# Turning every second pass of a GLU round and keeping its last weights in SBUF, in a kernel that runs attention and GLU side by side

## The chip, the cores and the metric

One core of a Trainium2 chip runs the kernel. The metric is the device time of one execution in microseconds (us), the median of several runs. The core has five engines with queues of their own: TensorE (PE) for matmuls, VectorE (DVE), ScalarE (ACT), GpSimd (POOL), and SyncE (SP), which here issues nearly all DMA transfers. Each engine works its queue in the order in which the kernel wrote the instructions.

## What is computed

The input x has 2048 tokens of 576 values. It is normalised (layer norm without weights), and goes through two branches that meet at the end:

```python
xn = _layernorm(x)
q, k, v = heads(xn @ wqkv)                      # 32 heads of 18
s = softmax(q @ k.T * 18 ** -0.5) @ v           # per head
s = join(s) @ wo
h = (xn @ w_gate) * (xn @ w_up)                 # 4608 wide
g = silu(h @ w_down)
return x + s * g
```

All of it is float32. The kernel splits each factor of a product into a part that the fast float32 form of the matmul holds and a rest, and adds three products (high by high, rest by high, high by rest).

## The kernel before

**Stages.** A first stage of some 300 us makes xn, q, k and v and puts them into DRAM scratch. A last one of some 75 us multiplies by wo and joins the branches. Between them, for some 2400 us, the scores of 32 heads and the whole GLU run interleaved on TensorE. The change touches this stage alone.

**The GLU.** It goes in four passes (`NCH`), one for each 512 tokens. A pass takes the 4608 hidden columns in 18 units (`NF2`) of 256; `units` lists the 72 pairs of pass and unit. A unit has two gate/up tiles n = 2u and 2u + 1 of 128 columns (`gw`, 1152 KB each with gate, up, and their rests, two buffers) and one down tile (`dw`, 1152 KB, one buffer). In the first pass the raw weights are loaded, split by ACT and POOL and stored to scratch (`swg`, `swd`), in later ones the split tiles are loaded from there. `g_get(n + 2)` is called where tile n's gate product ends, `d_get(u + 1)` where unit u's down sums end, and both issue their load on SP at once.

x of a pass lies in SBUF as 18 blocks (`xg`, 4.7 MB in all). In the last gate/up tile of a pass each block is overwritten with the next pass's as soon as it was used for the last time, first in one half of the partitions, then in the other (`x_block`).

**Two streams.** TensorE's rows are used in two halves. Stream 0 works in rows 0 to 63: the up products, half of the down columns, and the score tiles that find the row maxima (`a_item`: 512 keys, then a maximum on DVE). Stream 1 works in rows 64 to 127: the gate products, the other down columns, and the transposed scores (`b_item`: then an Exp on ACT). `visit` puts the products of probabilities and v between them. `stream(r)` yields the matmuls of one stream in their fixed order: two gate/up tiles of 27 matmuls (`TERMS`), then the down sums of the unit before, 4 x 12 matmuls (`DTERMS`).

**The planner.** `order()` decides, while the program is written, in which order all this stands on TensorE's queue. It holds a clock for each stream (`clk`), the times at which DVE and ACT come free (`free`), at which PSUM banks come free (`banks`), and one model of the DMA queue (`queue`): `moved(start, size)` says when `size` MB will have landed, at 0.26 MB per us and 2 us more. `can_go` lets a matmul be written only where the plan has its data there: `loaded` (gate/up tiles), `downed` (down tiles), `there` (x blocks and the products h). What a stream may not do is filled with scores; the scores have due times by the plan's clock (`a_goal`, `b_goal`, `PACE`). Stores, loads of heads and other small transfers are in the model in part only. The plan's times are not in the program: TensorE simply waits where data is late.

**Silu.** Two sets of sums (`acc`) serve four passes. When the four 128-token tiles of a pass are summed up, each one's silu is queued in `later` as seven pieces: an Exp on ACT (`first`), an add on DVE (`second`), four reciprocals of 144 columns on DVE (`inverse`), and a product on POOL with a store to scratch (`last`). They share one buffer, so a tile's Exp needs the store before it. `small(now)` is asked at every step of the planner. It writes the next piece if 6 us of plan time have passed since the last one (`quiet`) and if the piece's engine is free within 0.1 us. Two passes later the sums are overwritten; there `down_end` calls `ready(sdone, ...)`, which writes all pieces that are still missing, one after the other, without asking.

Of the kernel before, what the change touches and what calls it, by code (L numbers as in the profile page):

```python
# [20 lines left out]
FT = mybir.dt.float32  # L21
# [19 lines left out]
def kernel(  # L41
# [10 lines left out]
    nc = tc.nc  # L52
# [6 lines left out]
    NCH = S // 512  # L59
    NF2 = F // 256  # L60
# [14 lines left out]
    swd = dram.tile([NF2, 128, 2, 2, 2, HALF], FT, name="swd")  # L75
# [74 lines left out]
    chores, later = [], []  # L150
# [15 lines left out]

    units = [(c, p) for c in range(NCH) for p in range(NF2)]
    graw, gw, draw, dw = {}, {}, {}, {}  # L170
    gdone, ddone = set(), set()

# [4 lines left out]
    def g_get(n):  # L177

        if n == 2 * len(units):
            u = n // 2 - 1  # L180
            dw[u] = wpool.tile([128, 2, 2, 2, HALF], FR, name="wdl", tag="wgu", bufs=2)
            nc.sync.dma_start(dw[u].bitcast(FT), swd[u % NF2])
            ddone.add(u)
        if n >= 2 * len(units):
            return
        f = n % (2 * NF2)
        w = gw[n] = g_tile()
        if n >= 2 * NF2:
            nc.sync.dma_start(w.bitcast(FT), swg[f])
            gdone.add(n)  # L190
            return
        if n not in graw:
            ready(gdone, n - 2)
        raw = graw.pop(n)

        def piece(b):
            nc.scalar.activation(w[:, b:b + 3, :], raw[:, b:b + 3, :], AF.Copy)  # L197
            nc.gpsimd.tensor_tensor(w[:, 9 + b:12 + b, :], raw[:, b:b + 3, :], w[:, b:b + 3, :].bitcast(FT),  # L198
                                    op=OP.subtract)

        def end():
            gdone.add(n)
            nc.sync.dma_start(swg[f], w.bitcast(FT))
            g_load(n + 2)

        chores.extend([(piece, (b,)) for b in (0, 3, 6)] + [(end, ())])
# [5 lines left out]
    def d_get(n):  # L212
        if n >= len(units) - 1:
            return
        p = n % NF2
        w = dw[n] = d_tile()
        if n >= NF2:
            nc.sync.dma_start(w.bitcast(FT), swd[p])
            ddone.add(n)
            return  # L220
        raw = draw.pop(n)

        def piece(k):
            nc.scalar.activation(w[:, k, :, 0, :], raw[:, k], AF.Copy)  # L224
            nc.gpsimd.tensor_tensor(w[:, k, :, 1, :], raw[:, k], w[:, k, :, 0, :].bitcast(FT), op=OP.subtract)  # L225

        def end():
            ddone.add(n)
            nc.sync.dma_start(swd[p], w.bitcast(FT))
            d_load(n + 1)  # L230

        chores.extend([(piece, (k,)) for k in range(2)] + [(end, ())])
# [236 lines left out]
    with ExitStack() as mid:  # L469
# [148 lines left out]
            return acc[k][t % 4]  # L618

        def down_end(r, u, s, ps):  # L620
            c, p = units[u]
            cs = slice(r * HALF, (r + 1) * HALF)
            if p == 0 and c >= 2:
                ready(sdone, 4 * c - 8 + s)
            a = sums(4 * c + s)[:, cs]
            if p == 0:
                nc.vector.tensor_copy(a, ps[:, 0:HALF])  # L627
            else:
                nc.vector.tensor_tensor(a, a, ps[:, 0:HALF], op=OP.add)  # L629
            if p == NF2 - 1 and c < NCH - 1:  # L630
                seen[c, s] = seen.get((c, s), 0) + 1
                if seen[c, s] == 2:
                    silu_store(4 * c + s)
            if s == 3:
                seen[u] = seen.get(u, 0) + 1
                if seen[u] == 2:
                    d_get(u + 1)
# [46 lines left out]
        def stream(r):  # L684

            for u in range(len(units) + 1):
                for n in (2 * u, 2 * u + 1):
                    if u == len(units):
                        break
                    c, p = units[u]  # L690
                    box = []
                    for k in range(len(TERMS)):
                        def work(n=n, k=k, box=box, c=c, p=p):
                            if k == 0:
                                box.append(gu_start(r, n))
                            gu_op(r, n, box[0], k)
                            if p == NF2 - 1 and n % 2 and k % 3 == 2 and c < NCH - 1:
                                x_block(c + 1, k // 3, (64 * r,))
                                there["x", c + 1, k // 3, r] = moved(clk[r] + 0.5, 0.262)
                            if k == len(TERMS) - 1:  # L700
                                (gate_end if r else up_end)(n, box[0])
                                if r and n == 2 * len(units) - 1:
                                    wo_prepare()
                        end = (("DVE", 0.70) if r else ("ACT", 0.60)) if k == len(TERMS) - 1 else None
                        yield 0.229, k == 0, work, end, ("g", n, k)
                for s in range(4):
                    if not u:
                        break
                    box = []
                    for k in range(len(DTERMS)):  # L710
                        def work(s=s, k=k, box=box, u=u - 1):
                            if k == 0:
                                box.append(down_start(r, u))
                            down_op(r, u, s, box[0], k)
                            if k == len(DTERMS) - 1:
                                down_end(r, u, s, box[0])
                        end = ("DVE", 0.46) if k == len(DTERMS) - 1 else None
                        yield 0.131, k == 0, work, end, ("d", u - 1, 12 * s + k)
# [9 lines left out]
        clk, free = [0.0, 0.0], {"DVE": 0.0, "ACT": 0.0}  # L728
# [11 lines left out]

        def moved(start, size):

            queue[0] = max(queue[0], start) + size / 0.26
            return queue[0] + 2.0

        due, jobs, rows_done = [], [], {}
        there, queue = {}, [0.0]
# [54 lines left out]
        quiet = [0.0]  # L802

        def small(now):

            q = chores or later
            if q is later and now < quiet[0]:
                return
            if q:
                eng, length = KINDS.get(q[0][0].__name__, ("POOL", 0.0))  # L810
                if eng == "POOL" or free[eng] <= now + 0.1:
                    if eng != "POOL":
                        engine(eng, now, length)
                    if not chores:
                        quiet[0] = now + 6.0
                    chore()
# [39 lines left out]
        def can_go(r, first, ev):  # L856

            kind, n, k = ev
            now = clk[r]
            if kind == "d":  # L860
                return k or (there.get(("h", n), 1e9) <= now and (n < 1 or downed.get(n - 1, 1e9) <= now))
            u = n // 2
            c, p = units[u]
            if k == 0 and n > 1 and loaded.get(n - 2, 1e9) > now:
                return False
            if k == 0 and r and gone[0] - gone[1] < FIRST and heads[0] is not None:
                return False
            if k == len(TERMS) - 1:
                if r and upped.get(n, 1e9) > now + 0.3:
                    return False  # L870
                if not r and n > 1 and gated.get(n - 2, 1e9) > now + 0.3:
                    return False
            if c and p == 0 and n % 2 == 0:
                return there.get(("x", c, k // 3, r), 1e9) <= now
            return True

# [16 lines left out]
        def order():  # L893
# [5 lines left out]
            while any(heads) or na < TOTAL or nb < TOTAL or due or jobs:  # L899
                now = max(clk)  # L900
# [26 lines left out]
                elif op is not None:  # L927
# [8 lines left out]
                    if end:  # L936
                        done = engine(end[0], clk[r] + 0.22, end[1])
                        banks["g"][slots[r]] = done + 0.06
                        if kind == "d":
                            if k == 47:  # L940
                                parts.setdefault(n, []).append(clk[r])
                                if len(parts[n]) == 2:
                                    downed[n] = moved(max(parts[n]) + 0.3, 1.18)
                        elif r == 0:
                            upped[n] = done
                        else:
                            gated[n] = done
                            fin = engine("ACT", done + 0.1, 0.63)
                            loaded[n] = moved(done - 0.4, 1.18)
                            lands = moved(fin + 1.3, 0.524)  # L950
                            if n % 2:
                                there["h", n // 2] = lands
# [116 lines left out]
```

## Time and profile before

| | us |
|---|---|
| median of 3 runs (2808.34 to 2814.45) | 2813.01 |
| the profiled execution | 2809.35 |
| its span, first to last instruction | 2807.6 |
| PE busy | 2699.6 |
| DVE busy | 1966.2 |
| ACT busy | 1497.9 |
| POOL busy | 438.2 |

The profile is that of one execution. Busy is the time in which an engine had at least one instruction at work; matmuls of the two streams overlap, so TensorE can be busy with one stream as with both. A number behind an x is a count of instructions. PEclk is TensorE's granted clock as a share of 2.4 GHz, DMA the mean busy share of the 16 DMA engines. The DMA engines moved 522.87 MB, 186 GB/s over the span.

### The profile page before, as it was taken

To read this page: it belongs to the slowest core of one execution; us is meant where nothing else is said; L and a number is where in the kernel's file an instruction comes from. 1 tells how busy PE (TensorE), PEld (TensorE's weight loads), DVE (VectorE), ACT (ScalarE), POOL (GpSimd) and SP (SyncE) were. 2 spreads that over 40 slices of the span, in tenths; PEclk is the share of its full clock that TensorE was granted. 3 is DMA by queue.
4 is the path that set the end of the run, shared out by engine and by line. 5 is a ranking of instruction groups with operands and counts; after the bars stand their busy time and mean duration, and the time that the engine had idled before them with its cause. 6 is when DMAs were issued, how large, how long until landed. Compare 5 with 4: busy or idle time off the path is not lost.

```text
span 2807.6 us, 59270 instructions
## 1 busy us (share of the span) xinstructions
PE 2699.6 (96%) x24600; PEld 2165.5 (77%) x24600; DVE 1966.2 (70%) x3362; ACT 1497.9 (53%) x2765; POOL 438.2 (16%) x405
## 2 busy tenths in 40 slices
PE   7988999999999999999988999999988999999999
PEld 6876877777867877778766777777866777777769
DVE  6214777777767777777766777777767777777436
ACT  3221366666655555556554555555544555555642
POOL 2101433333320001001001000010001000100105
PEclk9998999999999999999998999999998999999989
DMA  7768978789786656565684555565685555654446
GB/s 233 262 198 247 249 213 220 209 217 244 212 225 176 174 157 181 155 182 165 164 212 132 172 162 169 158 174 161 185 203 154 157 166 162 189 157 147 156 144 207
DMA packets 210990, 522.87 MB, mean 186 GB/s; under 512 B 67200, under 2 KB 128672, under 8 KB 176160
## 3 DMA queue, kind: packets, MB, share of 16 engines
q1 hardware_dynamic: 208480, 510.82, 64.3%
q0 software_dynamic: 2240, 8.26, 0.8%
q8 instruction: 193, 3.16, 0.5%
q14 instruction: 77, 0.63, 0.1%
HBM read 330.17 MB, written 112.79 MB: 158 GB/s over the span
## 4 chain that ended last, share of the span: by engine, by line
PE 88%; DMA 7%; DVE 2%; SPq 1%; issue 1%; ACT 0%; POOL 0%; POOLq 0%; ACTq 0%; DVEq 0%
PE pg L573 32%; PE pg L532 16%; PE pg L601 14%; PE pa L487 12%; PE pb L521 7%; PE pg L1026 2%; DMA xc<-sx 2%; DMA wgu<-swg 2%; PE pa L318 1%; PE pg L373 1%; PE pb L318 1%; PE pb L547 1%; DMA qs<-sqk 1%; DVE xn L280 1%; DMA sqk<-hl 0%
## 5 line engine op out<-in xcount | busy, mean ns | idle before, releaser
L573 PE MATMUL pg<-xc,wgu 64*128 64x512 f32 x7776 | 1636.8, 395 | 41.6 <-DMA wgu<-swg 17.8
L523 ACT ACTIVATE pt<-pb 128x512 f32<-128x512 f32 x2048 | 1177.6, 596 | 740.2 <-PE pb L521 571.7
L489 DVE TENSOR_REDUCE mx<-pa 128x1 f32<-128x512 f32 x2048 | 1364.7, 686 | 206.3 <-PE pa L487 123.0
L573 PEld LDWEIGHTS pg<-xc,wgu 64*128 64x128 f32 x7776 | 1172.4, 188 | 99.7 <-DMA wgu<-swg 18.3
L601 PE MATMUL pg<-wd,hs 64*128 64x288 f32 x6816 | 1012.4, 295 | 14.0 <-DVE acc L627 14.0
L601 PEld LDWEIGHTS pg<-wd,hs 64*128 64x128 f32 x6816 | 946.7, 187 | 41.7 <-issue 16.2
L521 PE MATMUL pb<-qs,ks 56*128 56x512 f32 x2048 | 804.3, 409 | 7.1 <-DMA qs<-ml 5.5
L487 PE MATMUL pa<-ks,qs 54*128 54x512 f32 x2048 | 806.3, 405 | 0.8 <-DVE mx L489 0.6
L532 PE MATMUL pg<-pt,vt 128*32 128x512 f32 x4096 | 486.2, 602 | 6.4 <-ACT pt L523 6.3
L487 PEld LDWEIGHTS pa<-ks,qs 54*128 54x128 f32 x2048 | 371.8, 186 | 148.5 <-issue 111.1
L589 POOL TENSOR_TENSOR hs<-us,hs 128x512 fp32r<-128x512 f32 x144 | 185.7, 1290 | 1848.2 <-ACT hs L588 1767.4
L521 PEld LDWEIGHTS pb<-qs,ks 56*128 56x128 f32 x2048 | 365.5, 185 | 23.5 <-issue 5.6
L538 DVE TENSOR_TENSOR oc<-oc,pg 128x512 f32<-128x512 f32 x161 | 110.7, 687 | 335.9 <-PE pg L532 335.8
L532 PEld LDWEIGHTS pg<-pt,vt 128*32 128x32 f32 x4096 | 114.2, 110 | 245.9 <-issue 230.1
L629 DVE TENSOR_TENSOR acc<-acc,pg 128x288 f32<-128x288 f32 x544 | 240.4, 450 | 88.4 <-PE pg L601 74.8
L588 ACT ACTIVATE hs<-us 128x512 fp32r<-128x512 f32 x144 | 91.0, 632 | 154.6 <-DVE us L585 154.6
L198 POOL TENSOR_TENSOR wgu<-wraw,wgu 128x384 fp32r<-128x384 f32 x108 | 108.2, 1013 | 206.0 <-ACT wgu L197 183.6
L585 DVE TENSOR_TENSOR us<-pg,us 128x512 f32<-128x512 f32 x144 | 98.6, 685 | 20.6 <-PE pg L573 9.0
L578 ACT ACTIVATE us<-pg 128x512 f32<-128x512 f32 x144 | 85.9, 597 | 36.3 <-PE pg L573 31.6
L225 POOL TENSOR_TENSOR wd<-draw,wd 128x576 fp32r<-128x576 f32 x36 | 51.3, 1429 | 101.5 <-ACT wd L224 88.5
L1026 PE MATMUL pg<-wos,oT 128*128 128x288 f32 x448 | 63.1, 297 | 0.0
L1026 PEld LDWEIGHTS pg<-wos,oT 128*128 128x128 f32 x448 | 59.9, 188 | 0.3 <-ACT oT L1007 0.3
(99 smaller groups left out, 999.5 us busy)
## 6 DMA issues: line engine op xcount, KB each, us to landing
wgu<-swg SPq DMA_DIRECT2D x108, 1152.0 KB
hs<-hs SPq DMA_DIRECT2D x288, 256.0 KB
wd<-swd SPq DMA_DIRECT2D x53, 1152.0 KB
swg<-wgu SPq DMA_DIRECT2D x36, 1152.0 KB
qs<-sqk SPq DMA_DIRECT2D x192, 144.0 KB
ks<-sqk SPq DMA_DIRECT2D x192, 144.0 KB
swd<-wd SPq DMA_DIRECT2D x18, 1152.0 KB
sqk<-hl SPq DMA_DIRECT2D x32, 512.0 KB
```

Source lines behind the costliest of these rows:

```text
L198: nc.gpsimd.tensor_tensor(w[:, 9 + b:12 + b, :], raw[:, b:b + 3, :], w[:, b:b + 3, :].bitcast(FT), op=OP.subtract)
L487: nc.tensor.matmul(p, q[rows, t * 128:(t + 1) * 128], k[rows, c * 512:(c + 1) * 512], start=True, stop=True)
L489: nc.vector.tensor_reduce(mx[h][:, t, c:c + 1], p, axis=AX.X, op=OP.max)
L521: nc.tensor.matmul(p, k[rows, t * 128:(t + 1) * 128], q[rows, c * 512:(c + 1) * 512], start=True, stop=True)
L523: nc.scalar.activation(pt[t, c // 2][:, c % 2, :], p, AF.Exp, scale=scale)
L532: nc.tensor.matmul(p[32 * c:32 * c + 32, :], vt[h // 2][:, t, h % 2, :], pt[t, c // 2][:, c % 2, :], start=t == ts[0], stop=t == ts[-1])
L538: nc.vector.tensor_tensor(oc[h], oc[h], p, op=OP.add)
L573: nc.tensor.matmul(ps, gw[n][half[r], a, :], xg[i][half[r], e, :], start=k == 0, stop=k == len(TERMS) - 1)
L589: nc.gpsimd.tensor_tensor(hj[:, 1, :], h32, hj[:, 0, :].bitcast(FT), op=OP.subtract)
L601: nc.tensor.matmul(ps[:, 0:HALF], hs[u][half[r], k, j, a, s * 128:(s + 1) * 128], dw[u][half[r], k, j, e, :], start=n == 0, stop=n == len( ...
L629: nc.vector.tensor_tensor(a, a, ps[:, 0:HALF], op=OP.add)
L1026: nc.tensor.matmul(ps[h][:, 0:HALF], oc[:, e, :], w[:, h * HALF:(h + 1) * HALF], start=n == 0, stop=n == len(PAIRS) - 1)
```

## The change

Three things are edited. Odd passes take the columns from the last to the first (`columns_of`), so that a pass begins with the columns with which the one before ended; the two gate/up tiles and the down tile of that unit are not loaded again but taken over (`gw[n] = gw[n - 2]`, `dw[n] = dw[n - 1]`), and the planner is told so (0.0 for `loaded` and `downed`). `small` lets a silu piece in when its engine is free within 0.1 us plus 0.15 us for each us that the piece is past the 6 us. `moved` reckons with 0.24 MB per us. In the diff, `p` is renamed `q` where it is the place in the pass; those lines are cut, and so are the unchanged lines around.

```diff
-    units = [(c, p) for c in range(NCH) for p in range(NF2)]
+    units = [(c, q) for c in range(NCH) for q in range(NF2)]
+
+    def columns_of(u):
+        c, q = units[u]
+        return NF2 - 1 - q if c % 2 else q
+
...
-            nc.sync.dma_start(dw[u].bitcast(FT), swd[u % NF2])
+            nc.sync.dma_start(dw[u].bitcast(FT), swd[columns_of(u)])
...
-        f = n % (2 * NF2)
+        f = 2 * columns_of(n // 2) + n % 2
+        if n > 1 and n // 2 % NF2 == 0:
+            gw[n] = gw[n - 2]
+            gdone.add(n)
+            return
         w = gw[n] = g_tile()
...
-        p = n % NF2
+        p = columns_of(n)
+        if n and n % NF2 == 0:
+            dw[n] = dw[n - 1]
+            ddone.add(n)
+            return
         w = dw[n] = d_tile()
...
-            queue[0] = max(queue[0], start) + size / 0.26
+            queue[0] = max(queue[0], start) + size / 0.24
             return queue[0] + 2.0
...
-                if eng == "POOL" or free[eng] <= now + 0.1:
+                if eng == "POOL" or free[eng] <= now + 0.1 + (0.15 * (now - quiet[0]) if q is later else 0.0):
...
-                                    downed[n] = moved(max(parts[n]) + 0.3, 1.18)
+                                    downed[n] = moved(max(parts[n]) + 0.3, 1.18) if (n + 1) % NF2 else 0.0
...
-                            loaded[n] = moved(done - 0.4, 1.18)
+                            loaded[n] = moved(done - 0.4, 1.18) if (n // 2 + 1) % NF2 else 0.0
```

## Rows read from the trace of the kernel before

**Rows 1.** Page, engines (busy us, share, count) and chain that ended last:
```profile
PE 2699.6 (96%) x24600; PEld 2165.5 (77%) x24600; DVE 1966.2 (70%) x3362; ACT 1497.9 (53%) x2765; POOL 438.2 (16%) x405
...
PE 88%; DMA 7%; DVE 2%; SPq 1%; issue 1%; ACT 0%; POOL 0%; POOLq 0%; ACTq 0%; DVEq 0%
```
**Rows 2.** Engine time by stretch, undisturbed: length, busy (count) of each, clock, DMA:
```profile
400.00:800.00 400.00, 400.00 (x3872) 317.15 (x3873) 304.89 (x524) 272.50 (x509) 137.33 (x120) 1.00 0.82 221
...
1000.00:1400.00 400.00, 399.40 (x3838) 317.31 (x3835) 309.32 (x526) 230.96 (x412) 33.74 (x27) 1.00 0.58 166
1600.00:2000.00 400.00, 399.23 (x3858) 319.73 (x3856) 311.19 (x530) 230.41 (x412) 32.90 (x26) 1.00 0.59 167
```
**Rows 3.** Same view (PE, PEld, DVE, ACT, POOL), stretches with fewer matmuls:
```profile
800.00:872.00 72.00, 65.13 (x597) 47.66 (x591) 45.68 (x79) 36.33 (x66) 8.00 (x6) 0.95 0.89 218
1425.00:1497.00 72.00, 64.25 (x598) 49.78 (x594) 49.17 (x84) 37.36 (x67) 5.17 (x4) 0.95 0.76 182
1500.00:1572.00 72.00, 58.61 (x520) 45.48 (x521) 47.73 (x78) 32.07 (x57) 9.03 (x8) 0.88 0.51 146
2060.00:2132.00 72.00, 62.94 (x590) 48.72 (x590) 47.05 (x81) 35.96 (x65) 5.14 (x4) 0.95 0.80 195
2145.00:2217.00 72.00, 64.53 (x576) 49.10 (x572) 50.08 (x83) 34.49 (x62) 8.93 (x8) 0.88 0.49 145
2700.00:2735.00 35.00, 28.64 (x215) 22.28 (x213) 15.57 (x28) 8.12 (x20) 1.28 (x1) 0.76 0.40 119
```
**Rows 4.** Waits of TensorE's matmuls, whole span: us in total, times, longest:
```profile
PE pg L573 <- DMA wgu<-swg: 17.8, 4, 7.7
PE pg L601 <- DVE acc L627: 14.0, 2, 10.9
...
PE pg L532 <- ACT pt L523: 6.3, 1, 6.3
...
PE pg L573 <- DMA xc<-sx: 5.0, 5, 2.4
```
**Rows 5.** Chain that ended last, pieces at the disturbed stretches: start, us, what:
```profile
825.69 13.12 DMA wgu<-swg
...
1445.71 16.34 DMA wgu<-swg
...
1519.71 7.95 DMA sg<-sil
...
2084.30 13.02 DMA wgu<-swg
```
**Rows 6.** SP's queue in order of time, 1425 to 1452 us: start, us, issue:
```profile
1425.44 0.54 SPq L189 DMA_DIRECT2D wgu<-swg  x1
...
1445.71 0.49 SPq L189 DMA_DIRECT2D wgu<-swg  x1
...
1450.98 0.35 SPq L218 DMA_DIRECT2D wd<-swd  x1
```
**Rows 7.** Silu pieces (tile sil): DVE, ACT, POOL busy (count); waiters; reciprocals:
```profile
1000.00:1400.00 400.00, 8.20 (x9) 1.36 (x2) 4.15 (x4) 1.00 0.58 166
1600.00:2000.00 400.00, 7.75 (x8) 0.68 (x1) 2.01 (x2) 1.00 0.59 167
2600.00:2750.00 150.00, 11.35 (x12) 1.34 (x2) 6.05 (x6) 0.94 0.49 161
...
  PEld pa L487: 10.1, 12
...
L652 DVE RECIPROCAL sil<-sil x48: 993/1042/1053, 930.8 to 2738.7; 128x144 f32<-128x144 f32 x48
```
**Rows 8.** DVE in order of time, reciprocals at 1528 and 2155 to 2168 us:
```profile
1528.95 3.79 DVE L652 RECIPROCAL sil<-sil 128x144 f32<-128x144 f32 x4
...
2154.95 2.87 DVE L652 RECIPROCAL sil<-sil 128x144 f32<-128x144 f32 x3
...
2163.76 3.79 DVE L652 RECIPROCAL sil<-sil 128x144 f32<-128x144 f32 x4
```

More of the change, by code (lines that the diff above doesn't have):

```diff
@@ L620, in down_end @@
         def down_end(r, u, s, ps):
-            c, p = units[u]
+            c, q = units[u]
             cs = slice(r * HALF, (r + 1) * HALF)
-            if p == 0 and c >= 2:
+            if q == 0 and c >= 2:
                 ready(sdone, 4 * c - 8 + s)
             a = sums(4 * c + s)[:, cs]
-            if p == 0:
+            if q == 0:
                 nc.vector.tensor_copy(a, ps[:, 0:HALF])
@@ L629, in down_end @@
                 nc.vector.tensor_tensor(a, a, ps[:, 0:HALF], op=OP.add)
-            if p == NF2 - 1 and c < NCH - 1:
+            if q == NF2 - 1 and c < NCH - 1:
                 seen[c, s] = seen.get((c, s), 0) + 1
@@ L689, in stream, with work @@
                         break
-                    c, p = units[u]
+                    c, q = units[u]
                     box = []
                     for k in range(len(TERMS)):
-                        def work(n=n, k=k, box=box, c=c, p=p):
+                        def work(n=n, k=k, box=box, c=c, q=q):
                             if k == 0:
@@ L696, in work @@
                             gu_op(r, n, box[0], k)
-                            if p == NF2 - 1 and n % 2 and k % 3 == 2 and c < NCH - 1:
+                            if q == NF2 - 1 and n % 2 and k % 3 == 2 and c < NCH - 1:
                                 x_block(c + 1, k // 3, (64 * r,))
@@ L862, in can_go @@
             u = n // 2
-            c, p = units[u]
+            c, q = units[u]
             if k == 0 and n > 1 and loaded.get(n - 2, 1e9) > now:
@@ L872, in can_go @@
                     return False
-            if c and p == 0 and n % 2 == 0:
+            if c and q == 0 and n % 2 == 0:
                 return there.get(("x", c, k // 3, r), 1e9) <= now
```

## The prediction
> **What bounds the kernel now.** The page comes first: TensorE (PE) has work in 96% of the span and carries 88% of the chain that ended last, DMA 7% [rows 1]. So the time is TensorE's, unless TensorE itself is held. Being busy says little here, as a matmul counts as busy also when it streams beside another one or at half clock; so I count matmuls. Undisturbed, 3838 and 3858 run in 400 us [rows 2], that is 9.62 per us, or 693 in 72 us. Five stretches of 72 us fall short of that [rows 3]: 597, 598 and 590 at about 800, 1425 and 2060 us, and 520 and 576 at about 1500 and 2145 us. By count the first three lose 96 + 95 + 103 = 294 matmuls or 30.5 us, the other two 173 + 117 = 290 or 30.1 us: 60.6 us of 2807.6, and I see no other loss of that size between 300 and 2700 us.
>
> The first three are the ends of passes. The chain there runs through the loads of gate and up weights, 13 to 16 us from issue to landing [rows 5], and the waits name them (17.8 us) and the blocks of x (5.0 us) [rows 4]. The stretch of 1425 us shows the order on SP's queue [rows 6]: a weight load of 1.18 MB between the two halves of x, another right behind x, then the down weights. DMA moves 218, 182 and 195 GB/s there at shares of 0.89, 0.76 and 0.80 [rows 3], so about 0.24 MB per us when it is full: a weight load takes 4.9 us of the queue.
>
> The other two stretches come one unit later in passes 2 and 3. There the first down sums of a pass need the accumulator of two passes before, whose silu must be out. What is left of it is issued in one block on VectorE (DVE): 3.79, 2.87 and 3.79 us of reciprocals [rows 8], with two adds and a store of 7.95 us in the chain [rows 5]. TensorE waits 14.0 us for the accumulator copies behind them [rows 4], and the granted clock falls to a mean of 0.88, so that part of these 72 us runs at 1.2 GHz, not 2.4 [rows 3].
>
> **The change, part by part.** *Kept weights.* Three ends of pass lose two gate/up loads and one down load each: 9 x 1.18 = 10.6 MB less, and 9 issues less on SP (0.35 to 0.54 us each in [rows 6]). Nothing is added in their place: the same buffers are read, and the next load into them is issued one unit later, where every other unit has it. The weight wait of 17.8 us has no object left there. x is what can be late next: its second half moves up by the load ahead of it, 4.9 us at 0.24 MB per us, about the 5.0 us that TensorE waits for x now. The down load that goes stood behind x and gated nothing that the waits show. The columns that the backward pass reads second were stored units before, so no store is waited for.
>
> I put what stays at the ends at 8 us of the 30.5: the 5.0 us of x waits and about 3 us of half clock behind them. Bounds: 0, and 30.5 if x takes the place of the weights altogether. Gain 22.5 us.
>
> *Overdue silu.* Now a piece goes in only where the plan has its engine free within 0.1 us. With VectorE busy 309 of 400 us [rows 2] that gave 9 and 8 DVE pieces in 400 us [rows 7], while a pass needs 4 x 5 = 20 (and 8 on ACT and POOL) in some 620 us: hence the leftover. With 0.15 us of grace per us overdue, after 10 us a backlog of 1.6 us is let through, two of the score maxima. A piece then comes at the latest every 16 us or so; 28 x 16 = 448 us, less than a pass. So the two blocks should go: 30.1 us gained.
>
> What it costs: pieces that now stand in a block (11 reciprocals and 2 adds [rows 8]) and 12 at the end, where the score maxima are over [rows 7], move into the full stretches: 25 more. Their price there: pass 0, without silu, ran 3872 matmuls in 400 us, the next 3838 with 9 pieces and 3858 with 8 [rows 2, 7]: 3.8 and 1.8 matmuls a piece, 0.39 and 0.18 us. The work beside them hides the rest. I take 0.4, the dearer stretch, as denser pieces find less cover: 10 us. Bounds: 25 x 0.18 = 4.5 us, and 25 x 1.04 [rows 7] = 26 us if VectorE's time goes over whole to TensorE. Each Exp also waits on ACT for the store before it, with exps of the scores queued behind; POOL's mult (1.4 us) comes at least 6 us ahead in the plan, so 12 waits of 0 to 2 us, 0 to 24 us at the very worst; I take nothing for them, since ACT is the less loaded engine (231 of 400 us [rows 2]).
>
> At this place a rule of the Trainium skill speaks against the change. Behind 12 of the present pieces a weight load of TensorE stood, 10.1 us in all, 0.84 us each [rows 7]. The page "TensorE: Matmul & The Clock Gate" (section "Architectural detail: the array is 16× 32×32, not 1× 128×128") says that VectorE and ScalarE work their queues strictly in order, so a piece put in on a backlog holds every score maximum behind it. By that rule each piece would cost TensorE up to its whole length; that is the rival on the other side below. The trace bears it out for 12 of 60 pieces.
>
> *The planner's rate, 0.24 for 0.26 MB per us.* It issues nothing. A weight load is planned at 4.9 us, not 4.5, and x at 1.1, not 1.0. Only the ends of passes run without slack for that: elsewhere a load is issued about a whole tile of work before its use. It agrees with the 0.24 above. I take 0; since the written order shifts everywhere, from -5 to +8 us.
>
> *The end.* Attention is paced by the plan's clock, the GLU work fills in. If the GLU now ends sooner, exps are left alone. Today the two end together: [rows 3] shows 2700 to 2735 us with TensorE at 28.6 of 35 us and a 6.3 us wait for the last exps [rows 4]. 0 to +10 us; I take 0.
>
> **Sum.** -60.6 + 8 + 10 = -42.6 us on the profiled execution's 2809.35 us (span 2807.6), so 2766.8. The median of the runs, 2813.01, lies 3.7 above that execution; for a median I say 2770 us. Its own range is 2752 to 2789: all of both losses gone at the cheap price of a piece (-56 us, 2757, less 5 for a better order), or 20 us more left over.
>
> A second rule of the Trainium skill bears on the size. The matmul counts above say 60.6 us. "Trainium Kernel Development and Optimization" (section "Performance Expectations") calls matmul busy time a bad metric and wants the weight loads' busy share. The weight loads were busy 637.0 of 800 us, 57.3 of 72; the five stretches had 47.7, 49.8, 45.5, 48.7 and 49.1 [rows 2, 3], together 45.9 us less, 57.7 us at that share. By it the sum would be -39.7; by busy matmuls, whose idle is 44.5 us, only -26.5. The trace sides with the page.
>
> **Rivals.**
> - *x takes the place of the weights* (13%). The ends stay as long, since TensorE stops for x where it stopped for the weights. For: x waits already stand there. Against: x gets 4.9 us of queue. -30.1 + 10 = -20.1: 2793.
> - *The silu is not done in time* (6%): the grace never lets a piece in, and the blocks stay. For: VectorE's backlog is not shown for the plan. Against: 1.6 us of grace after 10 us. -30.5 + 8 = -22.5: 2790.
> - *Pieces cost their whole length, 1.04 us, in the 25 new places* (4%): -60.6 + 8 + 26 = -26.6: 2786.
> - *The tail* (5%): the GLU ends some 15 us before the exps, and these run alone. -42.6 + 15: 2785.
> - *Nothing to be measured* (5%): two of these together, with a worse order. 2813.
> - *Slower: VectorE becomes the bound* (9%). In the full stretches each of the 60 pieces, the careful ones of today too, holds a maximum, so a bank of scores, so TensorE's queue. Without the price of pieces the sum is -52.6, and 35 pieces already pay 0.4 = 14 us. Slower begins where 60 X - 14 = 52.6, X = 1.11 us a piece; at 1.04 + 0.84 = 1.88 us it is +46 us: 2859, at 1.3 us 2824. For: the 12 waits of 0.84 us. Against: 0.18 to 0.39 us a piece measured, and VectorE at 78%.
>
> The forecast has the remaining 58%. What this kernel's measurement can tell from no change is about 0.2%, 5.6 us. Faster is the forecast and the first four rivals, 86%; same 5%; slower 9%. The range for 8 in 10 is 2752 to 2800: the forecast's own and the four that lie between 2785 and 2793.
>
> **What would show it.** Right: 102 gate/up loads and 50 down loads where there are 108 and 53; over 650 matmuls in 72 us at each end of a pass and no wait for those weights; no block of four reciprocals at the first down sums of passes 2 and 3, no wait of TensorE for the accumulator copies; 12 or more DVE pieces of silu per 400 us, done well before the pass ends; full stretches at 9.5 or more matmuls per us. Wrong: x waits of over 5 us at an end; full stretches below 9.4 per us; maxima queued behind reciprocals in more than half of the cases; exps alone on ACT after 2660 us.

## The result and the profile after

The changed kernel takes 2767.76 us in the median of 4 runs (2765.33 to 2772.16), the kernel before in the same comparison 2811.62 (2808.34 to 2814.45): a ratio of 0.9846, 95% interval 0.9829 to 0.9863, 43.9 us less. The forecast was 2770. The profiled execution took 2772.16 us, with a span of 2770.4 us against 2807.6.

From the page of the changed kernel, the engines' line and two of the DMA issues (its lines for the GLU and the scores lie 15 further down: L588 is L573 of before, L616 is L601, L644 is L629):

```profile
PE 2686.6 (97%) x24600; PEld 2162.2 (78%) x24600; DVE 1952.3 (70%) x3362; ACT 1501.6 (54%) x2765; POOL 438.6 (16%) x405
...
wgu<-swg SPq DMA_DIRECT2D x102, 1152.0 KB
...
wd<-swd SPq DMA_DIRECT2D x50, 1152.0 KB
```

The same instructions run, six gate/up loads and three down loads are gone. Engine time by stretch of the changed kernel (columns as in [rows 2]): the three ends of passes at 800, 1395 and 2010 us, the first down sums of passes 2 and 3 at 1470 and 2100 us, a new loss at 2200 us, and three stretches of 400 us:

```profile
400.00:800.00 400.00, 399.00 (x3862) 314.45 (x3862) 303.63 (x521) 270.17 (x505) 136.85 (x120) 1.00 0.81 217
800.00:872.00 72.00, 71.01 (x673) 55.32 (x667) 51.90 (x90) 41.70 (x75) 8.01 (x6) 1.00 0.78 187
1000.00:1400.00 400.00, 397.23 (x3779) 313.57 (x3781) 307.85 (x526) 229.29 (x409) 33.66 (x27) 1.00 0.55 164
1600.00:2000.00 400.00, 396.32 (x3806) 309.19 (x3805) 307.31 (x528) 228.58 (x407) 36.90 (x30) 1.00 0.57 167
2200.00:2272.00 72.00, 64.46 (x597) 52.32 (x597) 49.13 (x84) 35.82 (x65) 7.13 (x6) 0.93 0.56 154
1395.00:1467.00 72.00, 71.85 (x692) 57.24 (x690) 54.88 (x95) 41.65 (x74) 5.16 (x4) 1.00 0.82 193
1470.00:1542.00 72.00, 71.87 (x703) 58.18 (x700) 58.70 (x101) 42.55 (x76) 7.99 (x7) 1.00 0.61 162
2010.00:2082.00 72.00, 72.00 (x695) 58.07 (x691) 56.26 (x96) 42.20 (x75) 6.45 (x5) 1.00 0.76 196
2100.00:2172.00 72.00, 72.00 (x697) 58.24 (x691) 56.48 (x96) 41.88 (x75) 7.16 (x6) 1.00 0.57 160
```

693 matmuls in 72 us was the undisturbed rate. The ends had 597, 598 and 590 [rows 3] and have 673, 692 and 695: 2 us are left of 30.5. The first down sums had 520 and 576 and have 703 and 697: nothing is left of 30.1. The granted clock stays at 1.00 in all five. Against that stand three losses. At 2200 us 96 matmuls are missing, 10.0 us. The stretches of 1000 and 1600 us ran 59 and 52 fewer than in [rows 2], 6.1 and 5.4 us. From 800 to 2600 us the changed kernel ran 17024 matmuls, the one before 16667: 357 more, or 37.1 us, which is the 37.2 us between the two profiled executions. The 43.9 us of the medians are more, as the profiled execution of the changed kernel lies 4.4 us above its median, the slowest of four, and that of the kernel before 2.3 below.

The waits of TensorE's matmuls over the whole span (us in total, times, longest):

```profile
PE pb L536 <- ACT pt L538: 8.7, 4, 7.5
...
PE pg L616 <- DVE acc L644: 8.6, 2, 6.8
PE pg L588 <- DMA xc<-sx: 5.6, 6, 2.7
...
PE pg L588 <- DMA wgu<-swg: 4.5, 2, 4.1
```

The 17.8 us for weights [rows 4] are 4.5, of which 4.1 lie within pass 1, not at an end. The accumulator wait that is left belongs to the last unit of all. The wait for x has not moved, and its place is why; the same view from 200 to 300 us:

```profile
PE pg L588 <- DMA xc<-sx: 5.4, 5, 2.7
```

It stands at the first load of x, ahead of pass 0. In the kernel before all 5.0 us lay there too.

The chain that ended last and ACT in order of time at the loss of 2200 us (start, us, what):

```profile
2215.78 1.39 POOL sil L670
...
2217.45 8.94 DMA sg<-sil
...
2227.07 0.59 ACT pt L538
```
```profile
2226.48 0.69 ACT L660 ACTIVATE sil<-acc 128x576 f32<-128x576 f32 x1 [10.32 <-DMA sg<-sil]
```

A silu tile's product and its store were followed on ACT by the next tile's Exp, which needs the same buffer. The store took 8.94 us, ACT stood for 10.32, and the scores' exps queued behind it held TensorE for 7.5 us. The kernel before had such waits too. First all of them in its span, then the longest, which stands in the silu block at 1500 us:

```profile
ACT sil L645 <- DMA sg<-sil: 30.4, 5, 10.1
```
```profile
1527.74 0.68 ACT L645 ACTIVATE sil<-acc 128x576 f32<-128x576 f32 x1 [10.07 <-DMA sg<-sil]
```

25.7 of the 30.4 us lie in the two blocks, beside the 10.5 us of reciprocals of [rows 8].

The pieces of silu in the changed kernel (DVE, ACT, POOL; counts):

```profile
800.00:1000.00 200.00, 9.27 (x10) 2.06 (x3) 4.15 (x4) 1.00 0.69 181
1000.00:1400.00 400.00, 9.28 (x10) 0.68 (x1) 4.02 (x4) 1.00 0.55 164
1600.00:2000.00 400.00, 9.26 (x10) 1.37 (x2) 6.06 (x6) 1.00 0.57 167
2200.00:2600.00 400.00, 10.31 (x11) 1.36 (x2) 6.01 (x6) 0.99 0.55 161
```

All 20 of a pass are out within some 350 us of its end, none in a block. Per 400 us they are 10, 10 and 11.

The end hardly changed. The last gate/up matmul and the first of the output stage of the changed kernel (first and last start, us):

```profile
L588 PE MATMUL pg<-xc,wgu x7776: 383/392/793, 233.4 to 2670.4; 64*128 64x512 f32 x200
...
L1041 PE MATMUL pg<-wos,oT x448: 290/294/399, 2696.6 to 2763.6; 128*128 128x288 f32 x150
```

26.2 us lie between the two, 34.4 (2699.9 to 2734.3) before. But from the last transposed score product (2666.8, before 2703.9) to the output stage it is 29.8 us and was 30.4. By count, 835 matmuls ran from 2600 us to the output stage, in 96.5 us, and 1188 in 134.2 before: 9.7 and 10.7 us short of the undisturbed rate, so some 1 us was gained there.

### The profile page after: what moved, and what is told of

Read it like the earlier page. It is cut to its first block, busy times and chain, and to the rows that moved or that the text cites. A ratio compares the mean times of both kernels' runs of the same rounds, so it can differ in the third digit from the quotient of the medians.

```text
span 2770.4 us, 59246 instructions
## 1 busy us (share of the span) xinstructions
PE 2686.6 (97%) x24600; PEld 2162.2 (78%) x24600; DVE 1952.3 (70%) x3362; ACT 1501.6 (54%) x2765; POOL 438.6 (16%) x405
## 4 chain that ended last, share of the span: by engine, by line
PE 87%; DMA 7%; DVE 3%; issue 1%; SPq 1%; ACT 1%; POOL 0%; POOLq 0%; DVEq 0%; ACTq 0%
PE pg L588 32%; PE pg L547 16%; PE pg L616 13%; PE pa L502 11%; PE pb L536 8%; PE pg L1041 2%; PE pa L333 1%; DMA xc<-sx 1%; PE pb L333 1%; PE pg L388 1%; DMA qs<-ml 1%; DMA wgu<-swg 1%; DVE mx L504 1%; PE pb L562 1%; DMA sqk<-hl 1%
## 5 line engine op out<-in xcount | busy, mean ns | idle before, releaser
L588 PE MATMUL pg<-xc,wgu 64*128 64x512 f32 x7776 | 1651.4, 394 | 20.4 <-DMA sv<-vo 8.7
L588 PEld LDWEIGHTS pg<-xc,wgu 64*128 64x128 f32 x7776 | 1181.5, 187 | 73.1 <-DMA xc<-sx 10.3
L616 PE MATMUL pg<-wd,hs 64*128 64x288 f32 x6816 | 1027.5, 293 | 0.0
L616 PEld LDWEIGHTS pg<-wd,hs 64*128 64x128 f32 x6816 | 961.4, 186 | 19.6 <-issue 7.7
L547 PE MATMUL pg<-pt,vt 128*32 128x512 f32 x4096 | 479.4, 597 | 1.3 <-DVE us L600 1.2
L644 DVE TENSOR_TENSOR acc<-acc,pg 128x288 f32<-128x288 f32 x544 | 241.4, 449 | 70.6 <-PE pg L616 60.2
L593 ACT ACTIVATE us<-pg 128x512 f32<-128x512 f32 x144 | 85.8, 596 | 28.8 <-PE pg L588 26.7
L551 ACT ACTIVATE oc<-pg 128x512 f32<-128x512 f32 x32 | 19.2, 600 | 79.9 <-PE pg L547 79.9
```

Source lines behind the costliest of these rows:

```text
L547: nc.tensor.matmul(p[32 * c:32 * c + 32, :], vt[h // 2][:, t, h % 2, :], pt[t, c // 2][:, c % 2, :], start=t == ts[0], stop=t == ts[-1])
L588: nc.tensor.matmul(ps, gw[n][half[r], a, :], xg[i][half[r], e, :], start=k == 0, stop=k == len(TERMS) - 1)
L616: nc.tensor.matmul(ps[:, 0:HALF], hs[u][half[r], k, j, a, s * 128:(s + 1) * 128], dw[u][half[r], k, j, e, :], start=n == 0, stop=n == len( ...
```

## The experiments

All are timed against the kernel before, in three groups; two kernels of different groups are compared by their medians.

| run | what it is | median us | ratio to before (95%) |
|---|---|---|---|
| e1_kept | turned passes and kept tiles alone | 2776.4 | 0.9877 (0.986 to 0.9895) |
| e2_grace | grace for silu alone | 2794.8 | 0.9942 (0.9921 to 0.9963) |
| e3_rate | 0.24 alone | 2818.2 | 1.0031 (1.0018 to 1.0044) |
| e4_no_rate | changed, with 0.26 | 2765.6 | 0.9833 (0.9813 to 0.9853) |
| e5_told_loads | changed, but tiles loaded again | 2821.9 | 1.0044 (1.0026 to 1.0062) |
| e6_kept_untold | changed, planner not told | 2795.0 | 0.9945 (0.9928 to 0.9963) |
| e7_three_recips | changed, 128 reciprocals more | 2979.0 | 1.0606 (1.0588 to 1.0624) |
| e8_wait_store | changed, 16 us after a store | 2761.5 | 0.9825 (0.981 to 0.984) |
| f1_untold_wait | e8, planner not told | 2760.8 | 0.9827 (0.9813 to 0.984) |
| f2_no_recips | e8 without 48 reciprocals | 2736.9 | 0.974 (0.9727 to 0.9754) |
| f3_wait_wo_026 | f4 with 0.26 | 2763.0 | 0.9836 (0.9819 to 0.9852) |
| f4_wait_wo | e8, wo's split later | 2755.5 | 0.9806 (0.9793 to 0.982) |

**The parts one by one.** Each takes some edits of the diff and leaves the rest as before; e4 is the changed kernel with this line:

```diff
-            queue[0] = max(queue[0], start) + size / 0.24
+            queue[0] = max(queue[0], start) + size / 0.26
```

> Turned passes and kept weights alone (planner told; silu strict, 0.26 as before). Theory that the parts add: the three ends of passes regain about 28 us, the two silu blocks stay with their 30 us, so about 2784 us, 0.990 of before; no wait for gate/up weights at the ends, the accumulator waits of 14 us still there. Rival that the end of the silu blocks alone gives the gain: 2811. Rival that the ends need the slower planned rate too, or x takes the weights' place: 2800 or more, with waits for x at the ends.

> Grace for overdue silu pieces alone (weights loaded again, 0.26). Theory that the parts add: the two blocks go (30 us), 25 pieces move into full stretches (10 us), and an Exp behind a store of silu can cost some 10 us as it did at 2217 us of the changed kernel: 2791, between 2780 and 2801 us. Rival that the blocks were made by the weight loads' disorder: 2811, the blocks still there.

> The planner's 0.24 MB per us alone. Theory: within 6 us of 2811.6, since it issues nothing and has slack but at the ends. Rival that the ends were late because the plan was too fast: the 7.7 and 7.6 us waits for gate/up weights go, and the time is 2795 or less.

> The changed kernel with 0.26 MB per us again. Theory that the rate does nothing: 2768 within 6 us, no weight waits at the ends. Rival that the rate keeps x from being late: 2780 or more, with waits of several us for x at the ends.

Kept tiles alone: 34.3 us less than the 2810.75 of the kernel before in the same group. Stretches of that kernel, one end of a pass and the two places of the blocks (the other ends, at 1440 and 2010 us, ran 620 and 690; the first of these reaches into a block):

```profile
800.00:872.00 72.00, 70.01 (x658) 53.57 (x657) 50.77 (x87) 41.13 (x74) 10.30 (x8) 0.98 0.80 199
...
1500.00:1572.00 72.00, 62.54 (x583) 48.51 (x582) 52.29 (x88) 35.07 (x64) 7.82 (x7) 0.95 0.52 154
...
2110.00:2182.00 72.00, 65.29 (x612) 51.44 (x610) 54.26 (x90) 37.83 (x68) 9.10 (x8) 0.95 0.52 153
```

The silu blocks stay, with as many pieces on DVE (17 from 1480 to 1600 and from 2080 to 2200 us, as before), but cost 110 + 81 matmuls, 19.8 us, not 30. What fell there is ACT's waiting for stores of silu, 12.5 us in place of 25.7; so those waits, more than the pieces, look like the cost of the blocks, though no run takes them out alone. Grace alone gained 15.9 us, 4 short of the middle of what was expected. The 10 us that it reckoned for an Exp behind a store did not come (4.8 us of such waits in its trace). Its stretches, two ends of passes and the two places of the blocks:

```profile
800.00:872.00 72.00, 63.79 (x580) 48.27 (x576) 44.59 (x77) 36.08 (x65) 8.16 (x7) 0.93 0.89 220
1425.00:1497.00 72.00, 64.36 (x585) 48.65 (x581) 44.41 (x77) 37.19 (x67) 5.18 (x4) 0.93 0.76 183
1500.00:1572.00 72.00, 71.95 (x689) 57.77 (x689) 58.96 (x100) 41.94 (x75) 7.16 (x6) 1.00 0.64 181
...
2145.00:2217.00 72.00, 71.08 (x684) 55.16 (x682) 56.74 (x98) 40.78 (x73) 7.11 (x6) 1.00 0.60 166
```

The ends keep their loss, the blocks are gone. So each part cures its own two or three places. 34.3 + 15.9 = 50.2 us, and both together without the rate (e4) 45.1: they add to within 5 us. The rate alone is no gain; with 2818.2 it also missed the 6 us that were expected. An end of a pass in e3 still falls short, with 533 matmuls (its profiled execution, 2829.5 us, was the slowest of twelve):

```profile
1440.00:1512.00 72.00, 62.86 (x533) 46.22 (x531) 43.20 (x72) 34.42 (x62) 5.12 (x5) 0.91 0.73 176
```

Three pairs differ by the rate alone. With 0.24 the time is 7.5 us more (e3 against before), 2.1 more (changed against e4) and 7.4 less (f4 against f3). It has no sign: what the three show is that a new order alone shifts this kernel by up to 8 us in such pairs.

**Bytes or order?** In e5 the branches that take the tiles over are cut, so that they are loaded; in e6 they stand, and the planner reckons with loads:

```diff
-                                    downed[n] = moved(max(parts[n]) + 0.3, 1.18) if (n + 1) % NF2 else 0.0
+                                    downed[n] = moved(max(parts[n]) + 0.3, 1.18)
...
-                            loaded[n] = moved(done - 0.4, 1.18) if (n // 2 + 1) % NF2 else 0.0
+                            loaded[n] = moved(done - 0.4, 1.18)
```

> The changed kernel, but the three tiles at each pass's start are loaded again from scratch, while the planner still takes them as there. Theory that it is the bytes and their place in the queue that made the ends late: the waits for gate/up weights come back, larger than before as the plan does not leave room for the loads, 8 to 15 us at each of three ends: 2790 to 2815 us. Rival that the plan's order made the gain: 2768 within 6 us.

> The changed kernel with the tiles kept, but the planner reckons as if they were loaded. Theory that the bytes count: 2768 within 8 us, since the plan only fills with scores what it need not. Rival that the planner must know: 2785 or more, with the up products of the ends written late and matmuls short there.

e5 lost 54.1 us against the changed kernel, a little over the upper end. TensorE's wait for weights (18.1, 13.4 and 3.4 us of it at the three ends), and two ends of passes:

```profile
PE pg L580 <- DMA wgu<-swg: 39.6, 4, 18.1
```
```profile
800.00:872.00 72.00, 52.88 (x486) 40.17 (x485) 36.69 (x65) 29.43 (x53) 7.98 (x6) 0.86 0.85 198
1440.00:1512.00 72.00, 57.14 (x535) 44.78 (x529) 42.62 (x73) 32.06 (x58) 5.16 (x4) 0.88 0.76 175
```

So the plan's order alone does not make the gain; without room in the plan, the bytes cost more than before. e6 was 27 us slower than the changed kernel, which spoke for the rival. But its chain named three stores of silu, each with an Exp behind it (ACT waited 10.8 us for the three):

```profile
991.54 8.91 DMA sg<-sil
...
2248.28 9.76 DMA sg<-sil
...
2321.16 9.40 DMA sg<-sil
```

That called for the wait in e8, and f1 then took both together:

```diff
-                        quiet[0] = now + 6.0
+                        quiet[0] = now + (16.0 if q[0][0].__name__ == "last" else 6.0)
```

> The changed kernel, but after a silu tile's product and store the planner waits 16 us, not 6, before it writes the next tile's Exp. Theory that the 8.94 us store in the chain at 2217 us is this Exp standing on ACT with the scores' exps behind it: no such stall, some 9 us regained: 2759 within 5 us. Rival that the order was only unlucky there and another stall takes its place: 2768.

> Tiles kept, the planner reckons as if they were loaded, and the planner waits 16 us after a silu store. Kept and untold alone took 2795 us. Theory that the plan's order at the ends costs it: matmuls there are still 73, 29 and 38 short in 72 us, so 12 to 15 us over the 2761.5 of the told kernel with the same wait: 2774 to 2777. Rival that its 27 us were Exps behind stores elsewhere: 2762 within 5 us.

e8 gained 6.3 us on the changed kernel, within what an order alone moves. But in its trace no Exp waits for a store, and from 2200 to 2600 us it ran 3841 matmuls where the changed kernel ran 3744: the 10 us there are back. f1 is as fast as e8: my theory for it fell. Untold, the ends of passes do run short:

```profile
800.00:872.00 72.00, 70.52 (x632) 54.02 (x626) 51.15 (x88) 41.67 (x76) 8.01 (x6) 0.98 0.73 185
...
1420.00:1492.00 72.00, 71.84 (x658) 54.98 (x656) 52.45 (x91) 41.59 (x75) 5.18 (x4) 1.00 0.70 161
```

TensorE is busy there, with scores in one stream, and the total is that of e8. What the order does ahead at an end is not to be done later: the last row maximum of f1 stands at 2562.0 us, that of e8 at 2579.5. So telling the planner was worth nothing between e8 and f1, and 27 us between the changed kernel and e6; every version that gained more than 16 us on the kernel before keeps the tiles. The 34 us between e6 and f1 came with the 16 us after a store. The three waits of e6, 10.8 us on ACT, are too short for them; the rest is a new order, and its cause is open.

**The price of a piece.** e7 makes each reciprocal three times; f2 is e8 without those of the passes:

```diff
-            later.extend([(first, ()), (second, ())] + [(inverse, (i,)) for i in range(4)] + [(last, ())])
+            later.extend([(first, ()), (second, ())] + [(inverse, (i,)) for i in range(4) for _ in range(3)] + [(last, ())])
```
```diff
-            later.extend([(first, ()), (second, ())] + [(inverse, (i,)) for i in range(4)] + [(last, ())])
+            later.extend([(first, ()), (second, ())] + [(inverse, (i,)) for i in range(4 if t >= 12 else 0)] + [(last, ())])
```

> The changed kernel with each reciprocal of silu in the passes and at the end made three times (the third gives the first's value again): 96 more DVE pieces of 1.04 us in the passes, and 32 more in the last stage, where they may stand in the chain for up to 33 us. Theory of 0.2 to 0.4 us a piece: 19 to 38 us in the passes, some more at the end: 2787 to 2840. Rival that a piece costs its whole length: 100 us in the passes alone, 2868 or more. Told apart by matmuls per us between 900 and 2500 us.

> The kernel that waits 16 us after a store (2761.5 us), without the 48 reciprocals of silu in the passes (silu's value is left out there; the last stage keeps its own). This gives their price. Theory of 0.2 to 0.4 us each: 2742 to 2752. Rival of the whole 1.04 us: 2711. Rival that their price rises with their density, as three reciprocals did (200 us for 128 more), and is nothing at this one: 2761.

f2 gives 24.6 us for 48 reciprocals, 0.51 us each if it is spread over all, above my 0.4 and half of 1.04. The stretches say that it must not be spread. Three stretches of e8, with 10, 11 and 12 silu pieces on DVE, then the same of f2, with none:

```profile
1000.00:1400.00 400.00, 397.04 (x3775) 311.95 (x3773) 306.57 (x525) 228.58 (x407) 33.64 (x27) 1.00 0.56 161
1600.00:2000.00 400.00, 399.69 (x3856) 319.32 (x3854) 312.87 (x537) 232.72 (x415) 36.97 (x30) 1.00 0.59 169
2200.00:2600.00 400.00, 399.51 (x3841) 317.00 (x3841) 297.19 (x511) 231.54 (x415) 37.00 (x30) 1.00 0.57 164
```
```profile
1000.00:1400.00 400.00, 398.55 (x3850) 316.30 (x3850) 301.58 (x519) 229.69 (x409) 30.98 (x24) 1.00 0.58 166
1600.00:2000.00 400.00, 399.76 (x3852) 323.18 (x3850) 303.84 (x521) 230.42 (x412) 31.06 (x24) 1.00 0.59 167
2200.00:2600.00 400.00, 399.84 (x3847) 316.30 (x3845) 282.52 (x484) 231.59 (x412) 31.04 (x24) 1.00 0.55 161
```

In the first stretch e8 runs 75 matmuls fewer, 7.8 us; in the other two 4 more and 6 fewer. Over the whole, 198 are missing from 800 to 1600 us, 20.6 us, and from 1600 to 2600 us none (9621 to 9614). So the pieces of the later passes cost nothing that counts, and the loss belongs to pass 1. There e8 waits for weights, from 850 to 1600 us:

```profile
PE pg L588 <- DMA wgu<-swg: 6.5, 3, 3.5
```

f2 has no such wait there. With the reciprocals gate tiles came to end close together (in e8 two loads are issued at 970.90 and 982.46 us), and the second's load was late. e4, the changed kernel with 0.26 (profiled in its fastest execution, 2757.7 us), has 30 pieces from 800 to 1600 us and ran 7668 matmuls there, e8 with 29 7494, f2 7692. So pieces need not cost this; it comes with the order in which they stand. 6.5 of the 20.6 us are waits for weights; the rest is not explained.

e7 went far beyond both theories: 211 us more than the changed kernel for 128 pieces. Of the 199.3 us between the two profiled executions 26.7 lie in the last stage, with 32 of the pieces; the 96 in the passes cost 172.6, 1.80 us each. Two stretches of it, the pieces in the second, and its longest wait:

```profile
1000.00:1400.00 400.00, 392.41 (x3705) 306.93 (x3704) 311.12 (x525) 223.84 (x398) 35.01 (x29) 0.99 0.56 161
1600.00:2000.00 400.00, 377.12 (x3494) 296.10 (x3488) 288.55 (x489) 196.49 (x357) 32.41 (x26) 0.97 0.54 155
```
```profile
1600.00:2000.00 400.00, 31.29 (x32) 1.35 (x2) 4.01 (x4) 0.97 0.54 155
```
```profile
PE pb L536 <- DMA qs<-ml: 56.0, 14, 9.5
```

Both stretches have 32 pieces, 22 more than in the changed kernel. The first lost 74 matmuls against it, 7.7 us or 0.35 us a piece, the second 312, 32.4 us or 1.5 us a piece. So the number of pieces in a stretch does not set the price alone. In the second VectorE's busy time does not rise (288.6 of 400 us), it falls: the score maxima came late, and the transposed scores waited for the row maxima of their head, which go over DMA, 14 times, 11 of them between 1400 and 2600 us. The last maximum was at 2790 us, against 2580 in the changed kernel. That a backlog of maxima builds up from stretch to stretch fits these numbers; no run shows it alone. It is not the path of my slower rival: that one held banks of scores, and TensorE's matmuls waited for a maximum (pa for mx) 0.5 us in all.

**The best version.** In the last unit accumulator adds stand on DVE behind the split of wo, which waits for its load. f3 and f4 hold that split back, beside the wait of e8:

```diff
+        wo_after = [0.0]
...
+            wo_after[0] = max(clk) + 12.0
...
-            if q is later and now < quiet[0]:
+            if q is later and now < quiet[0] or q is chores and now < wo_after[0]:
...
+        while chores:
+            chore()
```

> The changed kernel with the 16 us after a store, the split of wo written 12 us later so that accumulator adds don't stand on DVE behind wo's load (8.6 to 11.1 us of waits in the last unit), and 0.26 MB per us. Theory: 2761.5, less some 8 for wo, and 2 less for the rate: 2752. Rival that the last stage then waits for wo instead: 2760.

> The same with 0.24 MB per us. Theory: 2761.5 less some 8 us: 2753; the wait for accumulator adds in the last unit gone. Rival that the last stage then waits for wo: 2761.

TensorE's wait for accumulator adds, in e8 and then in f4:

```profile
PE pg L616 <- DVE acc L644: 11.1, 2, 8.7
```
```profile
PE pg L617 <- DVE acc L645: 5.2, 1, 5.2
```

f4 gains 5.9 us on e8, and that wait fell by 5.9; it did not go, as was expected. It beats both kernels: 2755.5 us, 12.2 less than the changed one. But f3, with 7.1 us of the same wait, came out at 2763.0, not 2752: no gain on e8. So that f4's gain comes from wo's split is not shown; it is no larger than what an order alone moves.

## Why the prediction was right, and where it was not

- *Where the time was lost*: right. 60.6 us were counted in five places, and after the change 2 us are left there. What held TensorE in the two blocks was read in part only: beside the reciprocals ACT stood 25.7 us for stores of silu. Counting matmuls found the size: idle time alone, 44.5 us, would have fallen short.
- *Kept weights*: right in its mechanism, shown by e1, e5 and f1. The 8 us that I left at the ends were 2. The step behind it failed: "the 5.0 us that TensorE waits for x now" was read from a row over the whole span, and all of it lay at 210 to 300 us. TensorE never waited for x at an end.
- *Overdue silu*: right in that both blocks go (e2). The price of a piece failed. I read 0.4 us off against the 3872 matmuls of pass 0; without any reciprocal f2 ran 3850, 3852 and 3847 in the later stretches, where the kernel before ran 3838 and 3858 with 9 and 8 pieces. So pass 0 was no yardstick, and the careful pieces cost about nothing. In the changed kernel 11.5 us are missing in the stretches of 1000 and 1600 us with only three pieces more than before; f2 and e4 say that this goes with the order, not with a price for each piece.
- *The Exp behind a store*: mis-sized. I put twelve waits at 0 to 2 us each and took nothing, as ACT is the less loaded engine. The trace before already had five, 30.4 us together, the longest 10.1. Load was the wrong measure: one wait of 10.32 us on ACT cost 10.0 us of matmuls, and in e8's trace they are back.
- *The end*: taken as 0, with 0 to +10 as bounds; by count it gave some 1 us.
- *The rate*: taken as 0, -5 to +8; measured +7.5, +2.1 and -7.4.
- *Sum*: -42.6 forecast for the profiled execution, where -37.2 came; the medians differ by -43.9. By count 58.6 of the 60.6 us came back, 6 more than the 52.6 that were reckoned, and 21.5 went again, the 10.0 at the store and 11.5 in the two full stretches, where 10 were reckoned for pieces. That the median lies within 3 us of 2770 is partly luck: terms were off by 6 and 11.5 us in opposite ways, and the spread between executions and a new order move the time by as much.
- *The signs*: the loads, the ends, the blocks and the accumulator copies came out as said. Two fell short: 10, 10 and 11 DVE pieces per 400 us, not 12, and 9.45 matmuls per us from 1000 us, not 9.5 (9.52 from 1600 us). How many maxima queued behind reciprocals was not counted.
- *Slower rival*: not here. e7 passed its break-even of 1.11 us a piece (1.80 in the passes), but by another path, and at one density the price was 0.35 us in one stretch and 1.5 in a later one.

## What to carry to other kernels

Find a loss by counting work done per us against an undisturbed stretch, and put each wait in its place by a window before a sum rests on it: a row over the whole span doesn't say where it stands. Where the order of passes is free, turn every second one and keep what is in SBUF. When optional work is spread into an ordered queue, look at what the queue does behind each piece, above all a piece that waits for a DMA: one Exp behind one store took 10.0 of the 21.5 us that the change gave back here. And measure what a piece costs by a kernel without it, stretch by stretch: an average over the whole hides where the cost lies.

## What was not expected of the hardware

A reciprocal of 1.04 us on VectorE had no fixed price. With 11 and 12 pieces per 400 us e8 ran as many matmuls from 1600 to 2000 and from 2200 to 2600 us as f2 with none; with 10 it ran 75 fewer from 1000 to 1400 us. With 32 per 400 us e7 lost 7.7 us in one stretch and 32.4 in a later one, though VectorE was never over 80% busy in any of these stretches (at most 312.9 of 400 us in e8's, 311.1 in e7's). The store of 288 KB in the chain took 8.9 us from issue to landing where heads and weights were loaded at the same time; the median of all twelve in the changed kernel was 4.2 us (2.6 to 8.9).
